# Eight small unread transfers on SP's DMA queue, behind two pieces of w_out and ahead of the first K load

## The chip, the core and the metric

The kernel runs on one core of one Trainium2 chip. The core has five engines with a queue of instructions each (TensorE or PE, VectorE or DVE, ScalarE or ACT, GpSimd or POOL, SyncE or SP) and 16 DMA engines that move data between HBM and SBUF. A DMA transfer is issued by an instruction on SP, ACT or POOL and is then carried out by DMA engines. The metric is device time in microseconds (us) of one execution, lower is better; the median of three runs stands for a kernel.

## The reference

Two blocks read the same normalised input and are added to it. All tensors are bf16.

```
xn  = layernorm(x)                                # x: 4 x 1 x 640
q   = xn @ wq                                     # wq: 640 x 4096, 32 heads of 128
p   = softmax(q . k_cache / sqrt(128))            # k_cache: 4 x 32 x 4096 x 128
A   = (p . v_cache) @ wo                          # v_cache like k_cache; wo: 4096 x 640
z   = gelu(xn @ w_in)                             # w_in: 640 x 1728, halves z1, z2
B   = (z1 * (w_sp * layernorm(z2) + b_sp)) @ w_out    # w_out: 864 x 640
out = x + A + B
```

The caches are 134 MB each. They are read once, and hardly anything is computed per byte.

## The kernel before

**Units.** The work is cut into 16 units: unit u is (g, b), with g one of four groups of 8 heads and b one of four batch rows. The K rows of one unit are 8 heads x 4096 keys x 128 values, 8.39 MB, laid out as 128 partitions x 64 KB; V likewise. `seq` lists the 32 loads: K of units 0 to 3, then V of u and K of u+4 in turn. `load_unit` (L180) issues them all on SP. They go into five half-unit slots of one tile `kv` (`place`), so a load can be issued only when what lay in its two slots has been used. Some loads are cut in two (`cuts`).

**Use of K and V.** For each K unit, DVE turns eight pieces with a stream transpose (L421) and PE multiplies them with q (L432). After four units of a group comes the softmax. For each V unit PE multiplies the probabilities with V (L505). At the end the last groups are projected with `wo` (`load_wo`, L188; `o_mul`, L548) and the result is stored (L616).

**The start.** SP issues, in this order: `wq` (L119, 5.24 MB into slots 0 and 1), `w_in` (L122, 2.21 MB), the first 384 rows of `w_out` (L126), then two pieces of the other 480 rows of `w_out` (`load_piece`, L132), then the first K unit (L180). The two pieces go into the tile `w_words`, which DVE first clears (L127), so they wait for that. The third piece is issued by POOL, behind a small transfer into a tile `walk` (L140) that nothing reads. ACT issues x, w_sp and b_sp (L113 to L116).

**Pieces and engines.** The large loads have 128 partitions, and each of the 16 DMA engines carries 8 of them. The pieces are narrower: piece 0 is 32 partitions of 7,680 B, piece 1 is 12 partitions of 17,920 B, and piece 2 is 8 partitions of 19,200 B. In the trace they land on 8, 3 and 2 engines.

**Semaphores of transfers.** Every transfer issued by SP or ACT counts on one of eight semaphores, here called lane 0 to lane 7. The framework hands them out in rotation, and a transfer that takes a lane again waits, on its issuing engine, until the lane's earlier transfer has landed. In the program before, the lanes of the start are:

```
lane 0  w_sp (ACT)     lane 4  w_in
lane 1  wq             lane 5  w_out, first 384 rows
lane 2  b_sp (ACT)     lane 6  piece 0
lane 3  x (ACT)        lane 7  piece 1
then again from lane 0: K unit 0 on lane 0, K unit 1 on lane 1, K unit 2 on lane 2, ...
```

In the program's listing, the K load of unit 0 waits for lane 0 alone. That of unit 1 waits for lane 1 (`wq`, whose slots it overwrites) and for POOL's `qT` (L311), that of unit 2 for DVE's reading of unit 0, whose slot it takes. SP works its queue strictly in order, so whatever waits there holds all later loads.

Of the kernel before, what the change touches and what calls it, by code (L numbers as in the profile page):

```python
# [12 lines left out]
BF16 = mybir.dt.bfloat16  # L13
# [3 lines left out]
def kernel(  # L17
# [19 lines left out]
    nc = tc.nc  # L37
# [35 lines left out]
    const = ctx.enter_context(tc.tile_pool(name="const", bufs=1))  # L73
# [56 lines left out]
    def load_piece(eng, t):  # L130
        p0, p1, n, k = PC[t]
        return eng.dma_start(out=w_rest[p0:p1, 0:n].rearrange("p c n -> p (c n)"),  # L132
                             in_=B_w_out[f_at[t]:f_at[t + 1], :].rearrange("(r i c) n -> i r (c n)", i=k, c=n))
# [3 lines left out]

    load_piece(nc.sync, 0)
    load_piece(nc.sync, 1)
    sw = nc.gpsimd.dma_start(out=walk, in_=B_w_out[0:14, 0:NST].rearrange("(r i) n -> i r n", i=7))  # L140
    with tc.issue_after(sw.ins):
        load_piece(nc.gpsimd, 2)
# [120 lines left out]
    for q in range(4):  # L263
        nc.gpsimd.tensor_copy(out=SelE[32 * q:32 * q + 32, :, q % 2, :],
                              in_=b8[32 * q:32 * q + 32, 8:8 + HP, None].to_broadcast((32, HP, P // HG)))
# [10 lines left out]
                          in_=ident_f[:].rearrange("p (q x c) -> p q x c", q=2, c=C2))  # L276
# [69 lines left out]
    for q in range(4):  # L346
        rows = slice(32 * q, 32 * q + 32)
        for m, (t, x0, x1, _) in enumerate(z_in[q]):
# [5 lines left out]
            else:  # L354
                for a in range(2):
                    nc.scalar.activation(out=dst[:, a].rearrange("p c (i r) -> p c i r", i=k),
                                         in_=z[:, a].rearrange("p (r i c) -> p c i r", i=k, c=n), func=ACT.Gelu_apprx_tanh)
# [287 lines left out]
```

## Time and profile before

| what | value |
|---|---|
| time, median of 3 runs | 663.27 us (663.25 to 663.32) |
| profiled execution, its own time | 663.23 us |
| its span, first to last instruction | 661.4 us |
| granted TensorE clock, mean | 0.724 |
| HBM read | 282.25 MB, 427 GB/s over the span |
| PE busy | 291.6 us, 44% |
| DVE busy | 376.6 us, 57% |
| ACT, POOL busy | 73.8 and 69.3 us, 11% and 10% |

The page's parts give the busy time of each engine, the span in 40 slices with the busy share of the DMA engines in tenths, the DMA queues, and the chain of work that ended last. The trace behind it also holds every packet that a DMA engine moved (start, duration, size, queue, but not the engine's number), and for every transfer the times at which each of its engines counted its share as landed.

### The profile page before, as it was taken

The page shows a single profiled execution, that of the slowest core. Times are in us where ns is not written, and L with a number is a line of the kernel's source. Part 1 is how long each engine was busy: PE and PEld are TensorE (multiplying, and loading weights), DVE is VectorE, ACT ScalarE, POOL GpSimd, SP SyncE. Part 2 cuts the span into 40 slices and gives each one's busy share as a digit, 9 for nine tenths or more (in the row PEclk, how much of TensorE's full clock was granted, in tenths as well). Part 3 has the DMA queues.
Part 4 walks back from the last instruction along what each step waited for, and adds up shares of the span by engine and source line. Part 5 has one row for each costly group of instructions (what it writes and reads, how often), then busy time and mean ns, then how long its engine had stood idle before and what let it go on. Part 6 is the DMA issues. An engine that isn't in the chain of part 4 may idle for free.

```text
span 661.4 us, 5465 instructions
## 1 busy us (share of the span) xinstructions
PE 291.6 (44%) x2269; PEld 109.5 (17%) x2269; DVE 376.6 (57%) x307; ACT 73.8 (11%) x143; POOL 69.3 (10%) x138
## 2 busy tenths in 40 slices
PE   0435665437063455225426075642607255641236
PEld 0211212112021121111202022210202112220013
DVE  4329999756191759718356186764619185971112
ACT  0300000331100000330200000070100000042200
POOL 3620000030200000130300000030110000002300
PEclk9869778768577697775858577665857658766678
DMA  8999999999999999999999999999999999999997
GB/s 367 458 433 436 417 434 446 437 424 433 428 437 440 432 413 437 437 433 444 425 424 436 433 416 451 434 425 436 432 437 444 417 432 423 434 444 441 409 424 288
DMA packets 7291, 282.60 MB, mean 427 GB/s; under 512 B 932, under 2 KB 1199, under 8 KB 1999
## 3 DMA queue, kind: packets, MB, share of 16 engines
q1 hardware_dynamic: 7127, 282.09, 99.0%
q8 instruction: 18, 0.29, 0.2%
q0 software_dynamic: 112, 0.16, 0.1%
q14 instruction: 6, 0.05, 0.0%
q10 hardware_dynamic: 28, 0.01, 0.0%
HBM read 282.25 MB, written 0.01 MB: 427 GB/s over the span
## 4 chain that ended last, share of the span: by engine, by line
DMA 76%; DVE 12%; issue 11%; PE 1%; SPq 0%; DVEq 0%
DMA kv<-in_A_k_cache_dram 65%; DVE w_words L421 11%; DMA kv<-in_A_v_cache_dram 9%; DMA kv<-in_A_wo_dram 1%; PE O L505 1%; DVE w_words L127 1%; SPq L132 0%; DVEq L421 0%; SPq L180 0%; PE last L548 0%; DVE o_bf L613 0%
## 5 line engine op out<-in xcount | busy, mean ns | idle before, releaser
L421 DVE STREAM_TRANSPOSE w_words<-kv 128x2048 f32<-128x2048 f32 x128 | 282.8, 2275 | 125.1 <-DMA kv<-in_A_k_cache_dram 125.1
L432 PE MATMUL S<-w_words,QZ 128*32 128x512 bf16 x1024 | 191.8, 509 | 254.1 <-DVE w_words L421 254.1
L432 PEld LDWEIGHTS <-QZ 128*32 128x32 bf16 x1024 | 60.8, 112 | 382.6 <-issue 320.1
L505 PE MATMUL O<-kv,Zb 128*32 128x512 bf16 x1024 | 74.2, 454 | 57.2 <-DMA kv<-in_A_v_cache_dram 43.3
L469 ACT ACTIVATE Zb<-w_words,MkE 32x128 bf16<-32x128 bf16 x120 | 60.8, 507 | 117.9 <-PE O L505 104.5
L514 DVE TENSOR_TENSOR om<-O,Mk 128x512 f32<-128x512 f32 x15 | 10.4, 692 | 94.4 <-PE O L505 94.4
L467 POOL TENSOR_SCALAR Zb<-w_words,MkE 32x128 bf16<-32x128 bf16 x60 | 42.9, 715 | 139.4 <-PE O L505 127.0
L505 PEld LDWEIGHTS <-Zb 128*32 128x32 bf16 x1024 | 34.3, 112 | 96.8 <-issue 68.5
L481 ACT ACTIVATE p_bf<-S,negmax 128x1024 bf16<-128x1024 f32 x4 | 4.5, 1114 | 400.8 <-DVE negmax L449 400.8
L465 DVE TENSOR_SCALAR Zb<-w_words,MkE 32x128 bf16<-32x128 bf16 x76 | 24.9, 328 | 2.3
L407 POOL COPY QZ<-qT 32x32 bf16<-32x32 bf16 x16 | 5.0, 315 | 184.7 <-PE S L432 184.1
L515 DVE TENSOR_REDUCE R<-om 128x128 f32<-128x512 f32 x15 | 15.3, 1021 | 0.5
L492 POOL TENSOR_SCALAR rs<-MkB,rowsum 128x4 f32<-128x4 f32 x4 | 1.2, 298 | 112.4 <-ACT p_bf L481 112.4
L487 DVE STREAM_TRANSPOSE w_words<-p_bf 128x1024 bf16<-128x1024 bf16 (+1 forms) x8 | 9.6, 1241 | 5.5 <-ACT p_bf L481 5.5
L538 POOL MEMSET oT<- 128x66 bf16 x4 | 0.5, 146 | 97.6 <-PE proj L548 97.6
L517 DVE TENSOR_SCALAR R<-O,Mk 128x128 f32<-128x128 f32 x1 | 0.4, 351 | 14.2 <-PE O L505 14.2
L439 DVE TENSOR_REDUCE m<-S 128x1 f32<-128x1024 f32 x4 | 4.9, 1224 | 5.6 <-PE S L432 5.6
L527 PE MATMUL misc<-R,SelX 128*128 128x512 f32 x8 | 4.5, 644 | 7.2 <-DVE R L515 5.5
L300 PE MATMUL q<-kv,xnT 128*32 128x512 bf16 x40 | 4.5, 629 | 6.6 <-DMA kv<-in_A_wq_dram 6.6
L494 PE MATMUL misc<-rs,SelE 128*128 128x4 f32 x8 | 2.2, 339 | 10.4 <-POOL rs L492 10.4
L548 PE MATMUL proj<-kv,oT 128*8 128x320 bf16 x52 | 5.5, 352 | 1.2 <-DMA kv<-in_A_wo_dram 0.6
L290 PE MATMUL proj<-kv,ident_bf 8*32 8x320 bf16 x2 | 0.7, 444 | 11.1 <-DMA kv<-in_A_x_dram 11.1
(105 smaller groups left out, 88.1 us busy)
## 6 DMA issues: line engine op xcount, KB each, us to landing
kv<-in_A_k_cache_dram SPq DMA_DIRECT2D x8, 4096.0 KB, 29.8
kv<-in_A_v_cache_dram SPq DMA_DIRECT2D x1, 6144.0 KB, 28.0
kv<-in_A_wq_dram SPq DMA_DIRECT2D x1, 5120.0 KB, 17.6
kv<-in_A_wo_dram SPq DMA_DIRECT2D x2, 1280.0 KB
kv<-in_B_w_in_dram SPq DMA_DIRECT2D x1, 2160.0 KB, 22.3
kv<-in_A_v_cache_dram SPq DMA_DIRECT2D x1, 2048.0 KB, 32.2
kv<-in_A_wo_dram SPq DMA_DIRECT2D x2, 640.0 KB
kv<-in_A_wo_dram SPq DMA_DIRECT2D x3, 320.0 KB, 23.0
```

The source lines that it names most:

```text
L127: nc.vector.memset(w_words[:, 0:FR * NOUT // 2], 0.0)
L407: nc.gpsimd.tensor_copy(out=QZ[r0:r0 + 32, :, :, :, 8 + 8 * hp], in_=qT[32 * g:32 * g + 32, NE * hp:NE * hp + NE].rearrange("p e a b -> p ...
L421: nc.vector.transpose(kT.rearrange("p (t r) -> p t r", r=32), kw)
L432: nc.tensor.matmul(S_ps[32 * q:32 * q + 32, i], lhsT=QZ[:, b, 2 * kh + w, e, w0:w0 + 32], rhs=kb[:, i, :, e, :, w], start=(b == 0 and k < ...
L465: nc.vector.tensor_scalar(out=dst, in0=src, scalar1=mk, scalar2=None, op0=ALU.mult)
L467: nc.gpsimd.tensor_scalar(out=dst, in0=src, scalar1=mk, scalar2=None, op0=ALU.mult)
L469: nc.scalar.activation(out=dst, in_=src, func=ACT.Copy, scale=mk)
L487: nc.vector.transpose(pT_t[:, j0:j1, :], blocks)
L505: nc.tensor.matmul(O_ps[32 * q:32 * q + 32, :, :], lhsT=Zb[b % 2][:, w].rearrange("p h c -> p (h c)"), rhs=vv[:, w * 4 * Dh:(w + 1) * 4 * ...
L514: nc.vector.tensor_tensor(out=om4[:], in0=O_ps[:], in1=Mk4[:, :, None].to_broadcast((P, 4, Dh)), op=ALU.mult)
L515: nc.vector.tensor_reduce(out=R, in_=om4[:].rearrange("p c d -> p d c"), axis=AX.X, op=ALU.add)
L548: nc.tensor.matmul(dst[0:nb, 0:n1 - n0], lhsT=state[("oT", g)][:, c0:c0 + nb], rhs=wo_t[g][:, c, n0:n1], start=start, stop=stop)
```

## The change

Behind the two pieces that SP issues, and ahead of the first K load, SP issues eight more transfers. Each copies the first r rows of `w_out`, 60 to 88 values of each row (120 to 176 B), into a new tile `mark` of 15 x 8 x 100 bf16, with r = 6, 7, 10, 11, 12, 13, 14 and 15. Nothing reads the tile. All of it together is 88 rows and about 13 KB.

```diff
     load_piece(nc.sync, 0)
     load_piece(nc.sync, 1)
+    mark = const.tile([15, 8, 100], BF16)
+    for i, r in enumerate((6, 7, 10, 11, 12, 13, 14, 15)):
+        nc.sync.dma_start(out=mark[0:r, i, 0:60 + 4 * i], in_=B_w_out[0:r, 0:60 + 4 * i])
     sw = nc.gpsimd.dma_start(out=walk, in_=B_w_out[0:14, 0:NST].rearrange("(r i) n -> i r n", i=7))
```

In the listing of the changed program, the order of instructions on PE, DVE, ACT and POOL is as before, line numbers moved by three. SP's queue reads as follows around the change, with the lanes that each waits for:

```
L132 piece 0                [DVE's clearing]
L132 piece 1
L142 mark  6 rows           [lane 0]
L142 mark  7 rows           [lane 1]
L142 mark 10 rows           [lane 2]
L142 mark 11 rows           [lane 3]
L142 mark 12 rows           [lane 4]
L142 mark 13 rows           [lane 5]
L142 mark 14 rows           [lane 6]
L142 mark 15 rows           [lane 7]
L183 K of unit 0            [lane 0]
L183 K of unit 1            [lane 1, POOL]
```

Eight transfers are one full turn of the eight lanes, so every later transfer keeps the lane that it had.

## Prediction

> **What bounds the kernel now.** I read the page's slices first, then its DMA queues and its chain.
>
> ```profile
> DMA  8999999999999999999999999999999999999997
> ...
> q1 hardware_dynamic: 7127, 282.09, 99.0%
> ...
> DMA 76%; DVE 12%; issue 11%; PE 1%; SPq 0%; DVEq 0%
> ```
>
> The DMA engines are full in every slice but the first and the last, nearly all of it on q1, SP's queue. The packets of the trace say it more sharply: from 2.43 to 656.62 us there is no gap of over 20 ns in which fewer than 16 packets are under way, and a 64 KB packet takes 2.42 us in 3,438 of 3,456 cases. So each DMA engine works down its own fixed list at a fixed pace, and the kernel ends when the last engine has ended its list. A pause of that engine is paid in full; a pause of another engine is paid only as far as that engine then becomes the last.
>
> How the end hangs on the last landing is seen in the chain of waits from 600 us on (start, length, what):
>
> ```profile
> 616.71 32.15 DMA kv<-in_A_v_cache_dram
> 648.86 0.02 issue
> 648.88 9.44 DMA kv<-in_A_wo_dram
> 658.32 0.04 issue
> 658.36 0.32 PE last L548 x4
> ```
>
> The last `wo` piece lands at 658.32; 3.1 us of arithmetic and storing follow to the span's end at 661.4. The second thing to see is at 648.86: the last `wo` load needs no data of the V load, it shares lane 5 with it, and SP issues it 0.02 us after that lane's landing. Lane waits do hold SP here.
>
> Third, SP's own queue in the first 60 us:
>
> ```profile
> 0.72 0.39 SPq L119 DMA_DIRECT2D kv<-in_A_wq_dram  x1
> ...
> 5.88 1.71 SPq L132 DMA_DIRECT2D w_words<-in_B_w_out_dram  x2
> 7.63 47.15 SPq L180 DMA_DIRECT2D kv<-in_A_k_cache_dram  x3
> ```
>
> The first K load is issued at 7.63 us, long before the engines need it (units 1 and 2 follow at 25.84 and 54.45). By the packets, the engines begin unit 0 at these times, in us:
>
> ```
> 7 engines without a piece                     20.92 20.94 21.01 21.05 21.21 21.38 22.24
> 4 engines with a share of piece 0 alone       22.23 22.27 22.28 22.32
> 5 engines with a share of piece 1 or piece 2  24.27 24.87 24.90 25.00 25.28
> ```
>
> **The change, part by part.** Nothing is removed. SP gets eight issues, each behind one lane. The landing events of before (last share of each transfer) are: w_sp 1.92, b_sp 7.94, x 11.02, wq 18.33, w_in 23.46, w_out 24.59, piece 0 25.40, piece 1 25.65. None of these depends on K, so they stay. SP then runs so:
>
> - mark 0 needs lane 0 (1.92) and goes out at 7.6. It stands behind piece 1 on the same queue; SP's transfers landed in the order of issue above, so it lands at about 25.7.
> - mark 1 needs lane 1, `wq`: SP stands until 18.33. Marks 2 and 3 follow at once.
> - mark 4 stands until 23.46, mark 5 until 24.59, mark 6 until 25.40, mark 7 until 25.65.
> - K of unit 0 comes behind mark 7. Its own lane's mark 0 has landed by then.
>
> An issue of so few rows isn't in the trace. The nearest rows are the 8-row store at L616 with 0.32 us, x (4 rows, L113) with 0.68, one value (L116) with 0.23, and the pieces with 0.88 and 0.78. I take 0.45, between the store and x; the ends are 0.23 and 0.88. Mark 6: 25.42 to 25.87; mark 7 to 26.33; K is issued at **26.35** (25.9 to 27.2).
>
> By then every ring is empty, so K meets 16 idle engines. The trace shows one such start, `wq`: issued at 0.72, first packets at 1.74 to 2.62, and the first packet of an engine lasts mostly 2.1 to 2.7 us instead of 1.51. Counted back from the end of `wq`, engines without other work behave as if they had begun 1.8 to 2.2 us after the issue, one of them 3.1. I take 1.9; the low end is 1.02, the first packet alone. So K runs as from **28.2** on all 16 engines (26.9 to 30.3). The five engines with the large pieces lose 3 to 4 us, the seven without a piece 6 to 7.
>
> [...]
>
> Which loss is paid? The early engines don't keep their lead: I followed each engine through the sorted landing offsets. The engines that begin K earliest are delayed now and then by about 1.5 us, whenever one of 17 packets of program code (16,384 B on q8, about 1.03 us, plus some 0.5 us on the packet behind it) falls to them. Eight engines take these in turn, six of them from the early group. The one whose share of unit 0 lands at 40.91 (start 21.21) takes the first, the ninth and the seventeenth (42.95, 328.22, 634.69 us), and it is **the one that ends last**, at 658.32. From its start on unit 0 to its end it needs 637.1 us, an engine with two such delays about 635.65, one with none 632.7. The pieces were lying on the engines with few code packets; the lead was being used up.
>
> With all engines starting together, the same engine ends last by a wider margin, and its loss counts whole: 28.2 - 21.2 = **+7.0 us**.
>
> What else could pay or cost: the marks' 88 packets are carried while the engines wait anyway (a 320 B packet takes 0.02 us, a 1,280 B one 0.055, so at most 8 x 0.064 = 0.5 us on one engine if that cover were missing). The later loads don't run dry: K of unit 2 goes out 9.2 us after unit 0 has landed (45.25 to 54.45); that becomes about 49.1 + 9.2 = 58.3, and units 0 and 1, 19.34 us each by their landings, keep the engines busy until 28.2 + 38.7 = 66.9. The spare is 8.6 us where the first engine had 20.9 + 38.7 - 54.45 = 5.2, since the landings spread less. DVE (57% busy) and PE shift along with the data. The tail of 3.1 us stays.
>
> Against the profiled execution's 663.23 us (span 661.4 and 1.8 around it; the median of the runs is 663.27) this gives **670.2 us**, 1.05% slower.
>
> **The rivals.**
>
> - *Only the late engines' loss is paid.* If the code packets fall differently (they begin their turn on other engines because the program has changed), the last engine could be one with a large piece and no code packets: 28.2 - 25.3 = +2.9, 666.1 us. For it: nothing fixes their first engine in what I see. Against: their number comes from PE's program, which is unchanged, and 17 over eight engines leave one engine with three anyway, whichever it is.
> - *No stall, so no change.* If the lanes did not hold SP, eight issues would put K's issue at 7.63 + 8 x 0.45 = 11.2 (14.7 at 0.88 each). The first engine needs it in its ring by 20.92 - 1.02 = 19.9; up to there the rings' backlog of `wq` and `w_in` hides it all. Price: 0 to 0.5 us for the packets, 663.2 to 663.7. Against it stand the listing's waits and the issue at 648.88 above. [...]
> - *A longer pause.* Marks at 0.88 us and a late start of the engine that ends last (3.1): 30.3 - 21.2 = +9.1, 672.3.
> - *Faster.* Eight engines, the last among them, end within 0.8 us, so no reshuffle of code packets gains 1.3 us, and a pause can't. Hardly possible.
>
> **How the numbers follow.** Forecast 0.76, late engines only 0.11, no stall 0.06, longer pause 0.05, faster 0.02. A difference of 0.2%, 1.3 us, is about what a measurement of this kernel can tell from no change. Faster 0.02; same 0.06 and a little for stalls smaller than I can see, 0.07; slower the rest, 0.91. The forecast's low end is K's start at 26.9 with the seventeenth code packet not counting: such an engine now starts unit 0 at 21.2 and must be 1.45 us later than now before it is last, so 26.9 - 21.2 - 1.45 = +4.3, 667.5. Its high end is 0.68 us a mark (K issued at 26.8) and a start 3.1 behind: 29.9 - 21.2 = +8.7, 671.9. Outside lie the late-engines case, no stall, faster, and most of the longer pause, about 2 in 10.
>
> **What would show it.** Right: SP's marks at about 7.6, 18.3, 18.8, 19.2, 23.5, 24.6, 25.4 and 25.9; the K load near 26.3; a hole of 2 to 6 us in the DMA packets between 21 and 28; unit 0's landings spread by about 1 us instead of 4.65; its last landing at 48 to 49 instead of 45.25; the last `wo` landing near 665.3, on one engine some 1.4 us behind the next. Wrong: K issued before 20 (then no change), or a last engine whose list has no code packets (then some 3 us).

## The result and the profile after

The changed kernel takes 670.40 us (median of four runs, 670.13 to 670.93) against 663.27 us: +7.1 us, ratio 1.0108 with a 95% interval of 1.0091 to 1.0126. It is slower, by nearly what was forecast. The profiled execution is the longest of the four, 670.93 us with a span of 669.1.

These are the lines of the page after that answer to those of before:

```profile
DMA  9799999999999999999999999999999999999996
...
q1 hardware_dynamic: 7303, 282.10, 98.0%
...
DMA 76%; DVE 12%; issue 11%; PE 1%; SPq 0%; DVEq 0%
```

The bytes are the same to 0.02 MB. The digit that has changed by more than one is that of the second slice (17 to 33 us): 7 instead of 9. By the packets nothing is lost behind that slice: from 28.64 to 660.99 us the engines are full again. The chain of waits at the end has kept its form, and its last landing (666.04 instead of 658.32) lies 7.7 us later:

```profile
622.09 34.55 DMA kv<-in_A_v_cache_dram
656.63 0.02 issue
656.65 9.39 DMA kv<-in_A_wo_dram
666.04 0.04 issue
666.08 0.32 PE last L551 x4
```

SP's queue in the first 60 us (start, length from the first to the last of the group, line) and, below, what SP waited for there (total us, times, longest):

```profile
7.63 19.12 SPq L142 DMA_DIRECT2D mark<-in_B_w_out_dram  x8
26.80 32.95 SPq L183 DMA_DIRECT2D kv<-in_A_k_cache_dram  x3
```

```profile
...
SPq L142 <- DMA kv<-in_A_wq_dram: 10.5, 1, 10.5
SPq L142 <- DMA kv<-in_B_w_in_dram: 4.1, 1, 4.1
...
SPq L142 <- DMA w_words<-in_B_w_out_dram: 0.8, 1, 0.8
SPq L142 <- DMA kv<-in_B_w_out_dram: 0.8, 1, 0.8
```

Eight transfers of 13 KB keep SP for 19 us. It isn't their own work: the marks, whose data nobody needs, wait for `wq`, `w_in`, `w_out` and piece 0, whose lanes they take over. In the trace each of the eight waits for the semaphore on which it then counts itself, and four go out 0.02 us behind the last landing there: at 18.59 (`wq` 18.57), 23.71 (`w_in` 23.69), 24.86 (`w_out` 24.84) and 26.02 (piece 0, 26.00). The K load behind them goes out at 26.80 instead of 7.63.

What this does to the DMA engines is seen in windows of 3 us (window, length, busy time of PE, its weight loads, DVE, ACT and POOL, then the granted clock, the DMA share and GB/s; a packet is counted where it starts, so the share can exceed 1). First the kernel before, then the one after:

```profile
21.00:24.00 3.00, 2.33 (x32) 0.94 (x26) 0.69 (x1) 0.40 (x1) 2.79 (x8) 1.00 1.22 523
24.00:27.00 3.00, 1.58 (x35) 1.32 (x30) 1.25 (x1) 1.71 (x4) 1.95 (x12) 1.00 0.92 398
```

```profile
21.00:24.00 3.00, 2.12 (x29) 0.92 (x23) 0.69 (x1) 0.37 (x1) 2.79 (x7) 1.00 0.43 179
24.00:27.00 3.00, 1.55 (x40) 1.28 (x30) 1.25 (x1) 1.75 (x4) 1.88 (x12) 1.00 0.10 34
```

The compute engines do much the same in both; what differs is the DMA columns. In the changed kernel five to ten engines still have a packet under way from 21.5 to 24 us, from 25.6 on hardly a packet runs, and the first K packets start at 27.81.

### The profile page after: what moved, and what is told of

It reads as the page before. It is cut to its first block, busy times and chain, and to the rows that moved or that the text cites. A ratio compares the mean times of both kernels' runs of the same rounds, so it can differ in the third digit from the quotient of the medians.

```text
span 669.1 us, 5473 instructions
## 1 busy us (share of the span) xinstructions
PE 292.3 (44%) x2269; PEld 110.2 (16%) x2269; DVE 376.6 (56%) x307; ACT 73.9 (11%) x143; POOL 69.3 (10%) x138
## 4 chain that ended last, share of the span: by engine, by line
DMA 76%; DVE 12%; issue 11%; PE 1%; SPq 0%; DVEq 0%
DMA kv<-in_A_k_cache_dram 62%; DVE w_words L424 11%; DMA kv<-in_A_v_cache_dram 10%; DMA w_words<-in_B_w_out_dram 3%; DMA kv<-in_A_wo_dram 1%; PE O L508 1%; DVE w_words L127 1%; SPq L142 0%; DVEq L424 0%; SPq L183 0%; PE last L551 0%; DVE o_bf L616 0%
## 5 line engine op out<-in xcount | busy, mean ns | idle before, releaser
L533 DVE TENSOR_TENSOR om<-misc,h 128x512 f32<-128x512 f32 x4 | 2.8, 692 | 4.9 <-PE misc L530 4.9
```

## The experiments

All compare with runs of the kernel before on the same chip, 663.24 to 663.26 us in the median. "Effective start" below is the time at which an engine would have begun its first 64 KB packet of K at full pace: the packet's end less 2.42 us. This makes up for first packets that last longer than usual.

**Three marks, four marks.** The same place, the list cut to its first three or four.

```diff
+    for i, r in enumerate((6, 7, 10, 11, 12, 13, 14, 15)[:3]):      # [:4] in the second
```

> Only the first three marks (6, 7 and 10 rows) stay at their place. Every transfer of SP and ACT waits for the one eight before it, so K of unit 0 now waits for x (landed 10.98) behind a mark that waits for wq (18.57); SP should issue it near 19.3. The first DMA engine runs out of work at 20.9, about 1.6 us later, and an issue needs about 1 us to its first packet. Lane theory: K is in the rings in time, 663.3 us (663.2 to 663.9). Rival, every mark costs its share of what eight cost (7.1 / 8 = 0.9 us each, by its packets or its issue): 663.3 + 2.7 = 666.0 us.

> The first four marks stay. Now K of unit 0 waits for w_in, which lands at 23.5 to 23.7, so SP issues it at 23.7; the engines without a piece are idle from 21 on, those with piece 1 or 2 are still busy until 24 to 25.6. Lane theory with the early engine's loss counted whole: effective start 23.7 + 2.1 = 25.8 against 21.2, +4.6, 667.9 us (667.0 to 668.5). Rival, only the loss of the late engines is paid: they go on almost without a gap, 663.3 to 664.0 us. Rival, 0.9 us a mark: 666.9 us, and evenly so from 3 to 4 marks (+0.9), where the lane theory has a jump of 4.6.

Measured: three marks 664.63 us (663.39 to 664.97; ratio 1.0018, 1.0009 to 1.0027), four marks 667.47 us (ratio 1.0064, 1.0052 to 1.0077). From three to four marks the time jumps by 2.8 us, against 1.4 from none to three. SP's waits with four marks:

```profile
SPq L142 <- DMA kv<-in_A_wq_dram: 9.9, 1, 9.9
SPq L183 <- DMA kv<-in_B_w_in_dram: 4.1, 1, 4.1
```

The second line is the K load itself (L183), waiting for `w_in`. It is issued at 23.09, and its effective start is 24.65 to 25.43 on the 16 engines. Engines with piece 1 or 2 are busy until about 24.3 to 25.3 in any case, so they lose less than a microsecond; those without a piece lose 25.0 - 21.2 = 3.8. The time grew by 4.2. So the loss of the early engines is paid, and that only the late ones' loss counts is ruled out. So is an even price of each mark: 0.9 us a mark would have made 666.0 with three marks, outside that run's interval (663.9 to 665.1).

With three or four marks every later load also takes another lane than before, since they are not a full turn of eight (with four, K of unit 0 takes that of `w_in`, the 4.1 us above). By the packets that costs nothing: from 26 us to 654 us no gap of over 20 ns has fewer than 16 packets under way in either profile.

Three marks cost more than I expected (1.4 us instead of at most 0.6). K is issued at 18.82, 2 us ahead of the first engine's running dry, and yet the packets show the engines not quite full: from 21.0 to 22.5 us between 12 and 15 packets are under way on average. The first K packets, begun at 20.85 and 21.09, last 3.44 us each. The effective starts of the early group are 21.9 to 22.7, some 3 us behind the issue. What I took for the lead that an issue needs (1 us) was too short. The eleven runs fall into two groups, three from 663.39 to 663.68 and eight from 664.48 to 664.97; the profiled one (664.86) is in the upper group, and what parts them isn't shown.

**Sixteen marks.** The eight twice, in a tile of 15 x 1184.

```diff
+    mark = const.tile([15, 1184], BF16)
+    m0 = 0
+    for i, r in enumerate((6, 7, 10, 11, 12, 13, 14, 15) * 2):
+        w = 60 + 4 * (i % 8)
+        nc.sync.dma_start(out=mark[0:r, m0:m0 + w], in_=B_w_out[0:r, 0:w])
+        m0 += w
```

> The eight marks twice, one behind the other (in a tile of other shape, 15 x 1184). The second eight wait for the landings of the first eight, which have landed by 28.0 at the latest, so hardly any further wait comes; there is only their issue, about 0.36 us each, now with nothing to cover it. Lane theory: K issued at 26.8 + 8 x 0.36 = 29.7, 670.4 + 2.9 = 673.3 us (672.5 to 674.5). Rival, each mark costs 0.9 us: 663.3 + 14.2 = 677.5 us. Rival, each further mark is a round trip of 1.3 us or more behind the one before: 681 us.

Measured: 673.42 us (ratio 1.0155, 1.0141 to 1.0169), 3.0 us over the eight.

```profile
7.61 21.50 SPq L144 DMA_DIRECT2D mark<-in_B_w_out_dram  x16
29.16 1.12 SPq L186 DMA_DIRECT2D kv<-in_A_k_cache_dram  x2
```

The second eight find their lanes free and go out every 0.34 to 0.43 us from 26.14 on; K follows at 29.16. With nothing to cover them, these marks cost the time of their issue, 3.0 / 8 = 0.38 us each. The first eight had cost 0.9 each because they had waited.

**The same eight, divided.** Two at their place, six behind the K load of unit 1.

```diff
     load_piece(nc.sync, 1)
+    marks(0, 2)
...
             load_unit(seq[i + 1])
+            if i == 0:
+                marks(2, 8)
```

> All eight marks on SP, but two at their place and six behind K of unit 1. Now K of unit 0 waits for b_sp and stands behind a mark that waits for wq: issued near 18.9, before the first engine runs dry. K of unit 1 stays behind POOL's qT (25.8). The six marks wait for w_in to piece 1 and the first two marks, all landed by 26.0, and K of unit 2 for unit 0, which it needs anyway. The packets and issues are the same 88 rows and eight instructions as in the changed kernel. Lane theory: 663.3 us (663.2 to 664.0). Rival, packets or issues of the marks cost: 670.4 us.

Measured: 663.82 us (663.70 to 664.78; ratio 1.0011, 1.0002 to 1.0020). The eight instructions and all their rows are there, and 6.6 of the 7.1 us are gone. SP's queue:

```profile
7.63 10.83 SPq L144 DMA_DIRECT2D mark<-in_B_w_out_dram  x2
18.52 7.52 SPq L187 DMA_DIRECT2D kv<-in_A_k_cache_dram  x2
26.08 2.40 SPq L144 DMA_DIRECT2D mark<-in_B_w_out_dram  x6
```

The six take 2.4 us in all and wait for nothing that hasn't landed. The 0.56 us that remain have two sources that fit: K still goes out at 18.52, a little late by what three marks showed (its early effective starts are 21.5 to 22.7), and the packets of the six marks (next run). Their shares aren't separated. Two of the eleven runs are longer, 664.59 and 664.78.

**Six or eight, behind unit 1.** None at their old place.

```diff
             load_unit(seq[i + 1])
+            if i == 0:
+                marks(2, 8)                  # marks(0, 8) in the second
```

> Six marks (10 to 15 rows) on SP behind K of unit 1, none ahead of K of unit 0. They take lanes 2 to 7, whose transfers have landed by 25.9, and K of unit 2 then takes lane 0, behind unit 0, for which it waits anyway. K of unit 0 is issued at 7.6 as in the kernel before. Lane theory: no wait that counts, 663.3 us (663.1 to 663.6). Rival, the half microsecond that the split kernel still lost was a cost of the marks' packets: six of them again 663.7 to 663.9 us.

> The same place behind K of unit 1, but all eight marks. The last two take lanes 0 and 1, on which K of units 0 and 1 are under way, so SP stands at the eighth mark until unit 1 has landed (64.6) and K of unit 2 is issued at 65.3 instead of 54.5. The engine that ends last runs dry at 61.8 and is fed again as from 65.3 + 2.1 = 67.4. Lane theory: +5.6, 668.9 us (667.5 to 670), against 663.3 with six. Rival, marks cost by their number or bytes: two more small ones (6 and 7 rows) cost nothing or little, 663.3 to 665 us.

Measured: six 663.56 us (663.46 to 663.81; ratio 1.0006, 0.9997 to 1.0015), eight 669.01 us (ratio 1.0087, 1.0073 to 1.0101). The two added ones are the smallest of all, 13 rows together, and cost 5.45 us. SP's waits with eight, and the window in which it stood at the last mark:

```profile
SPq L144 <- DMA kv<-in_A_k_cache_dram: 36.5, 2, 19.1
```

```profile
60.00:65.00 5.00, 2.24 (x16) 0.78 (x16) 3.24 (x3) 0.00 (x0) 0.00 (x0) 1.00 0.17 67
```

The last two marks, those of 14 and 15 rows, wait 36.5 us together for the K loads of units 0 and 1, whose lanes they take now that two more stand ahead of them; K of unit 2 goes out at 65.10. In the kernel before, the same 5 us move 433 GB/s. The hole was moved from 21 to 60 us by lanes alone.

Six marks cost 0.3 us, if anything (the interval of the ratio includes 1). Their packets stand between unit 1 and unit 2, from 59.6 to 64.4 us: on one engine about 0.1 us for the six, and the 64 KB packet that follows lasts 2.5 to 2.9 us instead of 2.42. In the kernel before, no packet from 55 to 70 us lasts over 2.44. From 63.6 to 64.1 us one engine has no packet under way at all, and why isn't shown.

**A late K load without marks.** POOL writes four values of `qT` where K of unit 0 will land, and the load stands behind that.

```diff
-    load_unit(seq[0])
...
     nc.gpsimd.tensor_copy(out=qT[:], in_=q4[:, 1, :]...)
+    nc.gpsimd.tensor_copy(out=at_slot(3, 4), in_=qT[:, 0, 0, :])
+    load_unit(seq[0])
```

> No mark at all. K of unit 0 is held in another way: POOL copies four values of qT into the place where this load lands, so that SP can issue it only behind qT, near 26.2. It is overwritten by the load, so nothing of the computation changes. Theory that the late issue is the whole cost: 26.2 + 2.1 - 21.2 = +7.1, 0.6 us less than the changed kernel's profiled run would give with its 26.8, 669.8 to 670.4 us. Rival, the marks themselves cost: 663.3 us, or the part of 7.1 that isn't theirs.

Measured: 669.87 us (669.61 to 670.10; ratio 1.0100, 1.0086 to 1.0114).

```profile
SPq L180 <- POOL kv L311: 18.4, 1, 18.4
```

K goes out at 26.01, 0.8 us ahead of the changed kernel's profiled run, with effective starts of 27.6 to 28.3 against 28.5 to 29.0. Without any mark, 6.6 of the 7.1 us are back; the difference is that of the issue. The hold alone makes the cost.

Put side by side (profiled executions; start is the middle of the 16 engines):

| kernel | K of unit 0 issued | effective start | time |
|---|---|---|---|
| four marks | 23.09 | 25.04 | 667.30 |
| hold alone | 26.01 | 27.9 | 669.90 |
| eight marks | 26.80 | 28.74 | 670.93 |
| sixteen marks | 29.16 | 31.32 | 673.51 |

From the first row to the last the start moves by 6.3 us and the time by 6.2. The start follows the issue by 1.9 to 2.2 us.

**More program code for PE.** The kernel before with 1,024 tiny matmuls added.

```diff
                 emit_K(u, k)
+                if k == 6:
+                    pad = misc_ps([32, 8], F32)
+                    for _ in range(64):
+                        nc.tensor.matmul(pad[:], lhsT=ident_bf[:, 0:32], rhs=ident_bf[:, 0:8], start=True, stop=True)
```

> The kernel before, with 1,024 tiny matmuls more on PE (64 for each K unit, 32x8, into a scratch tile that nothing reads), which makes PE's program longer by 2,048 instructions, some eight code packets of 16,384 B, one more for each of the eight engines that take them in turn. PE has idle time for them. Theory that a code packet on the engine that ends last is paid in full (about 1.0 us plus 0.5 us behind it): 663.3 + 1.5 = 664.8 us (664.4 to 665.3). Rival, these delays are covered by waits elsewhere and the end hangs on the late engines: 663.3 us.

Measured: 665.47 us (ratio 1.0034, 1.0020 to 1.0047), in five runs 664.82, 664.91, 665.47, 666.26 and 666.65.

```profile
q8 instruction: 26, 0.43, 0.3%
```

The page of before has 18 packets on q8. The median lies above the expected range (664.4 to 665.3). The two shortest runs give +1.6 and +1.7 us, what was expected of one more code packet on the last engine; the other three take 0.6 to 1.8 us more than these.

The trace of the profiled run (666.26) shows a second cost, which I had ruled out by saying that PE has idle time. From 126.1 to 131.7 us PE works on 190 of the added matmuls, and its work on V of unit 0 (L505), which began at 129.09 in the kernel before, begins at 131.56. SP waits for that work and issues V of unit 1 at 136.50 instead of 134.06. From 137 to 141 us there are then only 14 or 15 packets under way for most of the time, and 64 KB packets last up to 3.5 us: again a load that came too late to keep the engines full. Up to 655 us that is the only stretch of this kind but for one gap of 0.05 us. So the run doesn't measure the price of a code packet alone: the short runs agree with 1.5 us on the last engine, but the trace is of a long one, in which the late load has its part too.

## Why the prediction was right, step by step

- **Lanes hold SP.** Right. Marks were forecast at 7.6, 18.3, 18.8, 19.2, 23.5, 24.6, 25.4 and 25.9, and went out at 7.63, 18.59, 18.92, 19.25, 23.71, 24.86, 26.02 and 26.37. The one that differs most is mark 6: piece 0 landed at 26.00 here instead of 25.40. Of these 0.6 us, `wq`, `w_in` and `w_out` were already 0.2 late at their own landings; the rest isn't explained. In the trace the mark of 6 rows has 7 landing events and that of 15 rows 16, the first of each 0.5 to 0.6 us after the issue; what that first one counts isn't shown.
- **K issued at 26.35.** It went out at 26.80. The forecast was 0.6 us too early for mark 6's wait, and an issue of a mark took 0.28 to 0.43 us, not 0.45.
- **Idle engines: effective start 1.9 us after the issue.** Right: 1.9 to 2.2 in the four kernels of the table; their first packets came 1.0 to 1.3 us after the issue.
- **The early engine's loss counts whole, +7.0.** Measured +7.1 by the medians, +7.7 in the profiled pair. In that pair the terms can be read: the middle engine's start of 28.74 less 21.2 is 7.5, half a microsecond over the forecast, because K went out 0.45 us later than forecast. That the median comes within 0.2 us is in part luck; the path is not. The four-mark kernel shows directly that the early engines' loss is paid. Followed through the sorted landings as before, the engine with the first, ninth and seventeenth code packet (43.52, 331.11 and 640.64 us) again ends last; the margin to the next is 1.59 us, forecast 1.4.
- **No later dry spell.** Right: from 28.64 to 660.99 us there is no gap of over 20 ns with fewer than 16 packets under way (for the kernel before, the start of that stretch is 2.62, not 2.43). K of unit 2 went out at 59.42 (forecast 58.3).
- **Landings of unit 0: spread of 1 us, last at 48 to 49.** The fifteen others spread by 0.6 us and ended by 48.85; the last came at 50.20, since the first code packet (43.52) now falls into unit 0. I had placed it by its old time, behind that unit.
- **The rival without a stall** failed on its condition: the lanes do hold SP. Its price, and the sign "K issued before 20 (then no change)", also rested on a wrong threshold. K issued at 18.82 cost 1.4 us (three marks), and at 18.52 up to 0.56 (divided). The 1.02 us of lead were read off idle engines; behind busy ones these two runs show about 3.

None of these versions is faster than the kernel before.

## What to carry to other kernels

A transfer that nobody reads can still be the most expensive one in a queue, when it takes a semaphore whose last user hasn't landed: behind the K load of unit 1, eight marks cost 5.45 us more than six, and the last two had waited 36.5 us for units 0 and 1. Count back as many transfers as there are semaphores (eight here), and see what stands there. Put extra transfers where that one has landed anyway and where the loads behind them aren't due (six at that place: 663.56 us against 663.24). And where the DMA engines are always busy, ask which engine ends last and what it will still be delayed by: here the pause was paid by that engine (start some 7.5 us later, last landing 7.7), though it had begun unit 0 at 21.21, ahead of eleven of the sixteen.

## What the runs showed of the hardware

- A load issued 2 us before an engine ran dry didn't keep it at full pace: with three marks, issued at 18.82 us beside running transfers, K began in effect at 21.9 to 22.7 on the eleven engines that began it at 20.9 to 22.3 in the kernel before.
- Program code came through the same DMA engines: the page lists 18 packets on q8, "instruction", before and after, and 26 with 1,024 matmuls more on PE. In the profiles before and after they are of 16,384 B and last 0.9 to 1.1 us (but for the last one after, 1.4), and where a 64 KB packet stood behind one it lasted some 0.5 us longer (0.47 to 0.55). Followed through the landings, they fell on eight of the engines in turn.
- With six marks behind unit 1, a 64 KB packet behind a few rows of under 200 B lasted up to 0.47 us longer than 2.42.
- SP issued the second eight of sixteen marks, 6 to 15 rows with nothing to wait for, one every 0.34 to 0.43 us; they cost 3.0 us where nothing covered them.
